# Expert tiles gathered as 32-token blocks and turned by VectorE instead of TensorE

## The chip, the cores and the metric

The kernel runs on one core of one Trainium2 chip. The metric is the time of one execution in microseconds, measured on the device. The kernel before took 2295.74 us, the median of three runs from 2294.14 to 2295.92. One execution was also recorded by the hardware profiler; the rows below come from that record.

A core has a matrix engine (TensorE, PE in the rows; PEld is its weight load), a vector engine (VectorE, DVE), a scalar engine (ScalarE, ACT), GpSimd (POOL), and SyncE (SP), which issues most DMAs. Each engine takes its instructions in a fixed order.

## The reference

An attention without softmax feeds a mixture of experts.

```python
scores = z @ z.T / S                      # B = 8 batches, S = 2496, z is 64 wide
x = u * (relu(scores) ** 2 @ v)           # D = 256
logits = x @ w_gate + modality_bias[modality_id]
e = argmax(logits); gate = softmax(logits)[e]     # E = 8 experts, N = B * S = 19968 tokens
out[token] = gate * (relu(x[token] @ w1[e]) @ w2[e])      # w1[e]: 256 x 1024, w2[e]: 1024 x 256
```

Products are made in about fp32: each operand is split into a high part in the fp32r format and a low part, the rest, and three of the four partial products are added.

## The kernel before, in words

Phase 1 (to about 1358 us) is the attention: 400 steps of scores, square, split and product with v, ordered by a planner (`beside`) that places side work on ScalarE and VectorE by estimated costs and due times. Each token's row of 256 values, with its gate weight and its token number behind it (258 words), is scattered by GpSimd into `xs` in DRAM, where every expert has a region of its own. `lay_weights` copies w1 and w2 once into DRAM scratch (`w1s`, `w2s`) in the order in which a later load wants them.

Phase 2 is the experts, in tiles of 512 rows of one expert. Tiles are numbered from -4. Tiles -4 to -1 belong to the fullest expert, so that they can start before the last tokens are routed; tiles 0 to 34 follow, then a half tile. Tile -4 is turned at the end of phase 1, the three after it by the early tile ahead of them (tile 0 by tile -1), and tile t + 1 by tile t from then on: 39 whole tiles and one half are turned in all.

- `fetch(t)` loads the tile's rows from `xs` into a buffer of SBUF with one DMA; in tile t it loads tile t + 2. `fetch_weights` loads the expert's w1 and w2 behind it on SP.
- `turn(t)` brings features onto the partitions: per half of the features four TensorE transposes (`pt`, line 794) into PSUM, a ScalarE copy to the high part `xh` (line 802), a VectorE subtraction to the low part `xl` (line 803).
- `run_tile(t)` runs f = 0 to 7 over the hidden features in slices of 128. `up(t, f)` makes six matmuls of 512 columns into one of two PSUM buffers `ph` (line 952); then ScalarE makes `hh` (line 956) and VectorE `hl` (line 957), the high and low part after the relu. `down(t, f - 2)` follows `up(t, f)` from f = 2 on (lines 965, 966). The buffer that `up(t, f)` fills is that of `up(t, f - 2)`, so it waits until `hl` of f - 2 has read it. In tiles from 0 on, `turn(t + 1)` stands behind `up(t, 1)`; in early tiles behind `up(t, 5)`.
- `finish(t)` scales by the gate (`part`, `y`) and scatters rows of the output.

In phase 2 the order on every engine is the order of the code; in phase 1 SP's order is left to the scheduler of the language.

Of the kernel before, what the change touches and what calls it, by code (L numbers as in the profile page):

```python
# [21 lines left out]
def ins_of(x):  # L22
    return getattr(x, "ins", x)
# [3 lines left out]
def tile_attention_moe(ctx: ExitStack, tc: tile.TileContext, u, v, zt, mid, wg, mb, w1, w2, out):  # L27
# [11 lines left out]
    nc = tc.nc  # L39
    B, S, D = u.shape  # L40
# [30 lines left out]
    ident_r = const.tile([P, P], F32R, name="ident")  # L71
# [8 lines left out]
    turned = ctx.enter_context(tc.tile_pool(name="turned", bufs=1))  # L80
    rows = ctx.enter_context(tc.tile_pool(name="rows", bufs=1))
# [6 lines left out]
    def bank_tile(shape, name):  # L88
        return bank["pool"].tile(shape, F32, tag=bank["tag"], name=name)
# [29 lines left out]
    n = NCOL - J  # L119
# [16 lines left out]
    def make_blank():  # L136
        t = raw.tile([P, J, XW], F32, tag="blank", name="blank")
        nc.gpsimd.memset(t, 0.0)
        nc.gpsimd.memset(t[:, :, D + 1:D + 2], NOWHERE)
        blank.append(t)  # L140

    def clear(e):
        tc.keep_in_program_order(
            nc.sync.dma_start(out=xs[e * CAP:e * CAP + T, :].rearrange("(p j) c -> p j c", j=J), in_=blank[0])
        )
# [57 lines left out]

    def lay_weights(e, n):
        if n == 0:
            nc.sync.dma_start(out=w1s[e], in_=w1[e].rearrange("(k p) f -> p k f", p=P))
        else:
            nc.sync.dma_start(out=w2s[e], in_=w2[e].rearrange("(j p) d -> p j d", p=P))

# [128 lines left out]
    def evacuate_low(b, c, h):  # L338

        w = width[c]  # L340
        if not h:
            x = rows.tile([P, J, XW], F32, tag="x", bufs=NCH + 1, name="x")
            t = x.rearrange("p j c -> p (j c)")[:, 0:KD * T].rearrange("p (k t) -> p k t", k=KD)
# [147 lines left out]
    def scatter(b, k):  # L491
# [140 lines left out]
    G = len(steps)  # L632
# [20 lines left out]

    def none(f, *args):
        return (None, 0.0, f, args)
# [38 lines left out]
    for e in range(E):  # L694
        for n in range(2):
            k = 2 * e + n
# [16 lines left out]
    TL, W, head = {}, [None] * NW, []  # L713
    ready, fetched = {"n": 0}, {"n": 0}
    data = mybir.DependencyInfo(mybir.DependencyClass.Sync, mybir.DependencyReason.DATA)

    def wait_rows(i):
        for s in scatters[ready["n"]:]:
            tc.add_manual_dep(i, s.name, data, reason="rows of tokens")
        ready["n"] = len(scatters)  # L720

    def fetch(t, r0=0, nj=J):

        n = t + EARLY
        cell = first[0:1, 1:2] if t < 0 else meta[0:1, t, 0:1]
        row = nc.sync.value_load(cell, min_val=0, max_val=(E - 1) * CAP if t < 0 else E * CAP - T)
        k = fetched["n"] % 3
        fetched["n"] += 1
        xg = head[k // 2].tile([P, J, XW], F32R, tag=f"xg{k}", name="xg")[:, 0:nj, :].bitcast(F32)
        r0 += n * T if t < 0 else 0  # L730
        src = xs[bass.ds(row + r0 if r0 else row, nj * P), :]
        i = ins_of(nc.sync.dma_start(out=xg, in_=src.rearrange("(p j) c -> p j c", j=nj)))
        wait_rows(i)
        TL[t] = xg

    def weight_tiles(pool, n):
        W[n] = (
# [47 lines left out]
        if EARLY > 1:  # L785
            fetch(1 - EARLY)

    def turn_rows(t, dh):

        xg = TL[t]  # L790
        nj = xg.shape[1]
        pt = bank_tile([P, T], "pt")[:, 0:nj * P]
        for j in range(nj):
            nc.tensor.transpose(  # L794
                out=pt[:, j * P:(j + 1) * P].bitcast(F32R),
                in_=xg[:, j, dh * P:(dh + 1) * P].bitcast(F32R),
                identity=ident_r,
            )
        return pt

    def part_rows(x, dh, pt):
        nc.scalar.copy(out=x[0][:, dh, :], in_=pt)
        nc.vector.tensor_tensor(out=x[1][:, dh, :], in0=pt, in1=x[0][:, dh, :].bitcast(F32), op=ALU.subtract)

    def turned_tiles(nj):
        return [turned.tile([P, KD, T], F32R, tag="zm", bufs=NCH + 1, name=n)[:, :, 0:nj * P] for n in ("xh", "xl")]

    def turn(t):
        x = turned_tiles(TL[t].shape[1])
        for dh in range(KD):  # L810
            part_rows(x, dh, turn_rows(t, dh))
        TL[t] = (TL[t], *x)

    first_turned = []

    def turn_early(t):
        first_turned[:] = [turn_rows(t, dh) for dh in range(KD)]

    def part_early(t):
        x = turned_tiles(J)  # L820
        for dh in range(KD):
            part_rows(x, dh, first_turned[dh])
        TL[t] = (TL[t], *x)

    at(EG + 2, begin)
    for q in range(KD + 2):
        queue(G - 8 + q, G - 4 + q, act(1.05, part_weights_high, -1, q), dve(1.25, part_weights_low, -1, q))
    at(G - 5, turn_early, -EARLY)
    queue(G - 4, G - 4, none(part_early, -EARLY))

    ET = mybir.EngineType
    for c in range(3):
# [2 lines left out]
    with tc.manual_schedule(engines={ET.PE, ET.Activation, ET.DVE, ET.Pool}):  # L835
# [47 lines left out]
        for g in range(G):  # L883
            waiting += [(end, g, p) for end, p in due.pop(g, ())]
            b, c, i = steps[g]
# [6 lines left out]
            ahead = 1 + sum(g >= n for n in DEEPER)  # L892
# [77 lines left out]
    done = []  # L970

    def finish(t, po, group):
        xg, TL[t] = TL[t][0], None
        ids = mp.tile([P, J], I32, tag="ids", bufs=3, name="ids")[:, 0:len(po)]
        nc.vector.tensor_copy(out=ids, in_=xg[:, :, D + 1])
        mine = []
        for j in range(len(po)):
            gate = xg[:, j, D:D + 1]
            part2 = mp.tile([P, D], F32, tag="part2", bufs=2, name="part2")
            nc.scalar.mul(out=part2, in_=po[j][:, D:2 * D], mul=gate)  # L980
            y = mp.tile([P, D], F32, tag="y", bufs=6, name="y")
            nc.vector.scalar_tensor_tensor(out=y, in0=po[j][:, 0:D], scalar=gate, in1=part2, op0=ALU.mult, op1=ALU.add)  # L982
            i = ins_of(
                nc.gpsimd.indirect_dma_start(  # L984
                    out=out,
                    out_offset=bass.IndirectOffsetOnAxis(ap=ids[:, j:j + 1], axis=0),
                    in_=y,
                    in_offset=None,
                    bounds_check=N - 1,
                    oob_is_err=False,  # L990
                )
            )
            tc.declare_no_dep(i, group=group, reason="a tile's tokens are distinct")
            tc.add_to_no_dep_group(group, i)
            for s in done:
                tc.add_manual_dep(i, s.name, data, reason="rows that two tiles of an expert share")
            mine.append(i)
        done[:] = mine
# [5 lines left out]
                fetch(n)  # L1004

    def run_tile(t, ahead, extra={}, part=""):
        if not isinstance(TL[t], tuple):
            turn(t)
        po = [ps_o.tile([P, 2 * D], F32, tag="o", name="po") for _ in range(TL[t][0].shape[1])]
        h = {}  # L1010
        for f in range(KF + 2):
            if f < KF:
                h[f] = up(t, f)
            if 2 <= f < KF:
                for j in range(len(po)):
                    down(t, f - 2, h[f - 2], po, j)
            if ahead and t >= -1 and 2 <= f < 2 + KD + 2:
                part_weights_high(t + 1, f - 2)
                part_weights_low(t + 1, f - 2)
            for g in extra.get(f, ()):  # L1020
                g()
            if f == (1 if t >= 0 else 5) and ahead and t + 1 in TL:
                turn(t + 1)
        for j in range(len(po)):
            for f in range(KF - 2, KF):
                down(t, f, h[f], po, j)
        finish(t, po, f"out{t}{part}")
# [10 lines left out]
    for k, pieces in ((0, (route_logits, route_exp)), (1, (route_places,)), (3, (route_count,)), (4, (route_slots, route_gates))):  # L1038
        n, f = slots[k]
# [5 lines left out]
    n, f = slots[13]  # L1045
# [15 lines left out]
    if MAXT > UNC:  # L1061
# [49 lines left out]
```

## Time and profile before

| | |
|---|---|
| median of three runs | 2295.74 us |
| the profiled execution | 2293.02 us, span 2290.8 us |
| TensorE busy | 2263.6 us, 99% of the span |
| VectorE, ScalarE busy | 77%, 69% |
| granted TensorE clock, mean | 0.997 of full speed |

The span runs from the first to the last instruction; the execution's own time has 2.2 us around it. A busy TensorE is not one at its peak: matmuls are pipelined and their recorded ends overlap, so that what a matmul costs is read from the distance of two starts.

### The profile page before, as it was taken

Reading aid. Unit: us, or ns where it says so; the run is one execution under the profiler, and the core shown is the slowest. Engines: PE = TensorE matmul, PEld = TensorE weight load, DVE = VectorE, ACT = ScalarE, POOL = GpSimd, SP = SyncE. Lnnn points to the kernel's source line nnn. Section 1 sums busy time; section 2 is a strip of 40 time slices with the busy share of each in tenths; the row PEclk is TensorE's granted clock in tenths of the full one; section 3 lists DMA queues with packets and bytes.
Section 4 is the critical chain, followed back from the end, with each engine's and each line's share of the span. In section 5 each row is a group of like instructions: output and inputs, shape, how many; then the busy total and the mean of one; then the engine's idle time right before and its main releaser. Section 6 shows DMA issues by size and latency. Waiting matters only on the chain.

```text
span 2290.8 us, 44756 instructions
## 1 busy us (share of the span) xinstructions
PE 2263.6 (99%) x17220; PEld 2022.7 (88%) x17220; DVE 1758.0 (77%) x4540; ACT 1587.7 (69%) x1966; POOL 367.1 (16%) x350
## 2 busy tenths in 40 slices
PE   9999999999999999999999999999999999999996
PEld 7888888998998998999999998888888888888885
DVE  6879989989889889889889997656565555555563
ACT  8888888888888888888888863545454545444543
POOL 0000210210220210210211313112121212121211
PEclk9999999999999999999999999999999999999998
DMA  9602112112112112112110122534343434343430
GB/s 304 227 30 68 45 49 76 38 53 71 41 52 70 47 55 61 52 50 66 47 50 30 54 92 92 175 111 165 112 156 121 153 124 150 127 141 136 137 135 25
DMA packets 101791, 216.90 MB, mean 95 GB/s; under 512 B 15488, under 2 KB 63104, under 8 KB 96704
## 3 DMA queue, kind: packets, MB, share of 16 engines
q1 hardware_dynamic: 86432, 172.61, 23.1%
q0 software_dynamic: 15136, 41.34, 4.9%
q8 instruction: 137, 2.24, 0.4%
q14 instruction: 86, 0.70, 0.1%
HBM read 168.36 MB, written 62.32 MB: 101 GB/s over the span
## 4 chain that ended last, share of the span: by engine, by line
PE 92%; DVE 3%; ACT 2%; issue 2%; DMA 0%; POOL 0%; ACTq 0%; POOLq 0%; DVEq 0%
PE acc L305 42%; PE ph L952 18%; PE po L965 12%; PE s L265 11%; PE po L966 6%; DVE spare L385 1%; PE pt L794 1%; ACT r L267 1%; PE po L363 1%; ACT r L273 0%; DVE al L289 0%; ACT vh L234 0%; ACT x L347 0%; DMA out_dram<-y,ids 0%; DVE hl L957 0%
## 5 line engine op out<-in xcount | busy, mean ns | idle before, releaser
L267 ACT ACTIVATE r<-s 128x1024 f32<-128x1024 f32 (+1 forms) x400 | 403.4, 1008 | 198.3 <-PE s L265 187.6
L289 DVE TENSOR_TENSOR al<-r,ah 128x1024 fp32r<-128x1024 f32 (+1 forms) x360 | 431.0, 1198 | 101.6 <-ACT ah L280 85.1
L305 PE MATMUL acc<-ah,vh 64*128 64x512 f32 (+1 forms) x3120 | 465.7, 384 | 0.9 <-DVE ah L280 0.9
L385 DVE SCALAR_TENSOR_TENSOR spare<-x,wgb 128x256 f32<-128x256 f32 x1280 | 462.2, 421 | 1.0
L305 PE MATMUL acc<-ah,vl 64*128 64x512 f32 (+1 forms) x3120 | 458.5, 383 | 0.0
L956 ACT ACTIVATE hh<-ph 128x512 fp32r<-128x512 f32 (+1 forms) x320 | 189.8, 593 | 385.7 <-PE ph L952 376.4
L305 PE MATMUL acc<-al,vh 64*128 64x512 f32 (+1 forms) x3120 | 456.5, 382 | 0.1
L965 PE MATMUL po<-w,hh 128*128 128x512 f32 x1264 | 452.0, 393 | 0.0
L952 PE MATMUL ph<-xh,w 128*128 128x512 f32 (+1 forms) x1280 | 446.5, 395 | 0.4 <-issue 0.4
L273 ACT ACTIVATE r<-r 128x1024 f32<-128x1024 f32 (+1 forms) x400 | 416.3, 1041 | 3.5
L957 DVE SCALAR_TENSOR_TENSOR hl<-ph,hh 128x512 fp32r<-128x512 f32 (+1 forms) x320 | 219.1, 685 | 255.3 <-ACT hh L956 251.8
L305 PEld LDWEIGHTS acc<-ah,vh 64*128 64x128 f32 x3120 | 349.8, 184 | 27.5 <-ACT x L347 1.6
L305 PEld LDWEIGHTS acc<-al,vh 64*128 64x128 f32 x3120 | 350.1, 184 | 23.1 <-DVE al L289 0.5
L498 POOL DMA_INDIRECT xs<-x,sloti x160 | 205.5, 1284 | 1027.3 <-DVE x L496 939.2
L305 PEld LDWEIGHTS acc<-ah,vl 64*128 64x128 f32 x3120 | 347.3, 184 | 24.6
L265 PE MATMUL s<-zm 64*128 64x512 f32 (+1 forms) x2400 | 363.6, 387 | 4.9 <-ACT r L267 4.4
L966 PE MATMUL po<-w,hl 128*128 128x256 f32 x1264 | 353.4, 280 | 0.5 <-DVE hl L957 0.5
L280 ACT CAST ah<-r 128x1024 fp32r<-128x1024 f32 (+1 forms) x291 | 296.0, 1017 | 0.0
L952 PEld LDWEIGHTS ph<-xh,w 128*128 128x128 f32 x1280 | 239.5, 188 | 56.6 <-DVE hl L957 1.4
L965 PEld LDWEIGHTS po<-w,hh 128*128 128x128 f32 x1264 | 237.0, 187 | 55.1
L265 PEld LDWEIGHTS s<-zm 64*128 64x128 f32 x2400 | 260.3, 185 | 24.8 <-ACT r L267 7.5
L984 POOL DMA_INDIRECT out_dram<-y,ids x158 | 154.2, 976 | 725.4 <-DVE y L982 699.7
(138 smaller groups left out, 1967.1 us busy)
## 6 DMA issues: line engine op xcount, KB each, us to landing
w<-w1s SPq DMA_DIRECT2D x37, 1024.0 KB
w<-w2s SPq DMA_DIRECT2D x37, 1024.0 KB
xg<-xs SPq DMA_DIRECT2D x39, 516.0 KB
vr<-in_v_dram SPq DMA_DIRECT2D x32, 512.0 KB
ut<-in_u_dram SPq DMA_DIRECT2D x32, 512.0 KB
zr<-in_zt_dram SPq DMA_DIRECT2D x40, 256.0 KB
w1s<-in_moe_w_dram SPq DMA_DIRECT2D x8, 1024.0 KB
w2s<-in_moe_w_dram SPq DMA_DIRECT2D x8, 1024.0 KB
```

Of the source, the lines that this page charges most:

```text
L265: nc.tensor.matmul(out=s[:, t, :w], lhsT=lhs, rhs=mv[halves[t], ql, :w], start=n == 0, stop=n == 2)
L267: nc.scalar.activation(out=r[:, :, :w], in_=s[:, :, :w], func=AF.Relu, scale=INV)
L273: nc.scalar.square(out=a[:, :, :w], in_=a[:, :, :w])
L280: copy(out=ah[:, :, :w], in_=st_a[g][:, :, :w])
L289: nc.vector.tensor_tensor(out=al[:, :, :w], in0=a[:, :, :w], in1=ah[:, :, :w].bitcast(F32), op=ALU.subtract)
L305: nc.tensor.matmul(out=acc[b, c][r][dh][:, :w], lhsT=V[b, k // J][y][halves[r], k % J, dh * P:(dh + 1) * P], rhs=x[halves[r], k % 2, :w], ...
L385: nc.vector.scalar_tensor_tensor(out=spare[:, k % 2, :], in0=x[:, j, 0:D], scalar=1.0, in1=wgb[:, e, :], op0=ALU.mult, op1=ALU.mult, accum ...
L498: nc.gpsimd.indirect_dma_start(out=xs, out_offset=bass.IndirectOffsetOnAxis(ap=RT[b]["sloti"][:n, k:k + 1], axis=0), in_=x[:n, j, :], in_o ...
L952: nc.tensor.matmul(out=ph, lhsT=lhs, rhs=rhs[:, k, :], start=n == 0, stop=n == 3 * KD - 1)
L957: nc.vector.scalar_tensor_tensor(out=hl, in0=ph, scalar=0.0, in1=hh.bitcast(F32), op0=ALU.max, op1=ALU.subtract)
L965: nc.tensor.matmul(out=po[j], lhsT=hh[:, s], rhs=both, start=f == 0, stop=False, skip_group_check=True)
L966: nc.tensor.matmul(out=po[j][:, 0:D], lhsT=hl[:, s], rhs=w[:, 0, :], start=False, stop=f == KF - 1, skip_group_check=True)
```

## The change

Each tile is gathered by five DMAs. Four load blocks: features 64 b to 64 b + 63 of token 32 t + i go to partition 32 b + i, where block t has 64 words, so that one VectorE instruction, which turns every 32 x 32 square of a 128 x 1024 operand, leaves features on partitions and tokens in their order along the row. The fifth loads gate and token number into `side`. With this a partition holds other features than before (feature 64 b + 32 k + q on partition 32 b + q), and `lay_weights` orders the rows of w1 to match, in two copies of half the size. Three instructions take the place of `turn`'s twelve: a VectorE transpose `xt`, a ScalarE copy `xh`, and a VectorE subtraction `xl`, the last two now 1024 wide and from SBUF. They stand behind `up(t, 0)` (the first two) and `up(t, 1)` in tiles from 0 on, behind `up(t, 5)` and `up(t, 6)` in early ones, and the planner places those of tile -4.

```diff
     def lay_weights(e, n):
         if n == 0:
-            nc.sync.dma_start(out=w1s[e], in_=w1[e].rearrange("(k p) f -> p k f", p=P))
+            for k in range(KD):
+                nc.sync.dma_start(
+                    out=w1s[e, :, k, :].rearrange("(b q) f -> b q f", q=BLK),
+                    in_=w1[e].rearrange("(b k q) f -> k b q f", k=KD, q=BLK)[k],
+                )
...
-        src = xs[bass.ds(row + r0 if r0 else row, nj * P), :]
-        i = ins_of(nc.sync.dma_start(out=xg, in_=src.rearrange("(p j) c -> p j c", j=nj)))
-        wait_rows(i)
-        TL[t] = xg
+        src = xs[bass.ds(row + r0 if r0 else row, nt), :]
+        dmas = []
+        for b in range(P // BLK):
+            cols = slice(b * KD * BLK, (b + 1) * KD * BLK)
+            rows_of = src[:, cols].rearrange("(t i) c -> i t c", i=BLK)
+            dmas.append(nc.sync.dma_start(out=xg[b * BLK:(b + 1) * BLK], in_=rows_of))
+        dmas.append(nc.sync.dma_start(out=side, in_=src[:, D:XW].rearrange("(j p) c -> p j c", p=P)))
...
-    def turn_rows(t, dh):
...
-    def part_rows(x, dh, pt):
-        nc.scalar.copy(out=x[0][:, dh, :], in_=pt)
-        nc.vector.tensor_tensor(out=x[1][:, dh, :], in0=pt, in1=x[0][:, dh, :].bitcast(F32), op=ALU.subtract)
...
+    def turn_blocks(t):
+        side, xg = TL[t]
+        nt = xg.shape[1] * BLK
+        xt = turned.tile([P, KD, T], F32, tag="zm", bufs=NCH + 1, name="xt")[:, :, 0:nt]
+        TL[t] = (side, xt)
+        nc.vector.transpose(
+            out=xt.rearrange("p k (t i) -> p k t i", i=BLK), in_=xg.rearrange("p t (k c) -> p k t c", k=KD)
+        )
+    def part_high(t):
+        side, xt = TL[t]
+        xh, xl = (turned.tile([P, KD, T], F32R, tag="zm", ...)[:, :, 0:xt.shape[2]] for n in ("xh", "xl"))
+        nc.scalar.copy(out=xh, in_=xt)
...
+    def part_low(t):
+        side, xh, xl, xt = TL[t]
+        nc.vector.tensor_tensor(out=xl, in0=xt, in1=xh.bitcast(F32), op=ALU.subtract)
...
-    at(G - 5, turn_early, -EARLY)
-    queue(G - 4, G - 4, none(part_early, -EARLY))
+    queue(G - 6, G - 4, dve(1.2, turn_blocks, -EARLY), act(1.05, part_high, -EARLY), dve(1.25, part_low, -EARLY))
...
-            if f == (1 if t >= 0 else 5) and ahead and t + 1 in TL:
-                turn(t + 1)
+            if ahead and t + 1 in TL:
+                if f == (0 if t >= 0 else 5):
+                    turn_blocks(t + 1)
+                    part_high(t + 1)
+                if f == (1 if t >= 0 else 6):
+                    part_low(t + 1)
```

On ScalarE, in a tile from 0 on, the order before was (`part` is the end of the tile ahead, `hh` the slices f = 0, 1, 2 of this one):

```order
L980 ACTIVATE part_23309<-po,xg 128x256
L980 ACTIVATE part_23316<-po,xg 128x256
L956 ACTIVATE hh<-ph 128x512 x2
L802 CAST xh<-pt 128x512 x2
L956 ACTIVATE hh<-ph 128x512
L770 CAST w_0_18680<-w_0_18680 128x1024
```

and it is now:

```order
L982 ACTIVATE part_23213<-po,xg 128x256
L982 ACTIVATE part_23220<-po,xg 128x256
L958 ACTIVATE hh<-ph 128x512
L816 CAST xh<-xt 128x1024
L958 ACTIVATE hh<-ph 128x512 x2
L785 CAST w_0_18688<-w_0_18688 128x1024
```

`xh` of the next tile has moved from behind `hh` of f = 1 to ahead of it.

On VectorE, in the same place, the order before was (`y` is the end of the tile ahead):

```order
L982 SCALAR_TENSOR_TENSOR y<-po,xg,part_23316 128x256
L957 SCALAR_TENSOR_TENSOR hl<-ph,hh 128x512 x2
L803 TENSOR_TENSOR xl<-pt,xh 128x512 x2
L957 SCALAR_TENSOR_TENSOR hl<-ph,hh 128x512
L774 TENSOR_TENSOR w_0_18680<-w_0_18680 128x1024
```

and it is now:

```order
L984 SCALAR_TENSOR_TENSOR y<-po,xg,part_23220 128x256
L959 SCALAR_TENSOR_TENSOR hl<-ph,hh 128x512
L809 STREAM_TRANSPOSE xt<-xg 128x1024
L959 SCALAR_TENSOR_TENSOR hl<-ph,hh 128x512
L821 TENSOR_TENSOR xl<-xt,xh 128x1024
L959 SCALAR_TENSOR_TENSOR hl<-ph,hh 128x512
```

The transpose stands between `hl` of f = 0 and `hl` of f = 1, and `xl` between those of f = 1 and f = 2.

On VectorE at the end of phase 1 the order before was (`al` and `ah` are the attention's split, `spare` the router's products, `w` the low parts of tile -4's weights):

```order
L385 SCALAR_TENSOR_TENSOR spare,lg<-x,wgb 128x256 x4
L496 COPY x<-side 128x2
L803 TENSOR_TENSOR xl<-pt,xh 128x512 x2
L291 TENSOR_TENSOR al<-r,ah 128x448
L292 TENSOR_TENSOR al<-r,ah 64x448
L385 SCALAR_TENSOR_TENSOR spare,lg<-x,wgb 128x256 x6
L774 TENSOR_TENSOR w_0_18680<-w_0_18680 128x1024 x2
```

and it is now, from the transpose on:

```order
L809 STREAM_TRANSPOSE xt<-xg 128x1024
L391 SCALAR_TENSOR_TENSOR spare,lg<-x,wgb 128x256 x2
L295 TENSOR_TENSOR al<-r,ah 128x2x448
L391 SCALAR_TENSOR_TENSOR spare,lg<-x,wgb 128x256 x6
L502 COPY x<-side 128x2
L286 CAST ah<-r 128x2x448
L297 TENSOR_TENSOR al<-r,ah 128x448
L298 TENSOR_TENSOR al<-r,ah 64x448
L391 SCALAR_TENSOR_TENSOR spare,lg<-x,wgb 128x256 x2
L789 TENSOR_TENSOR w_0_18688<-w_0_18688 128x1024
L821 TENSOR_TENSOR xl<-xt,xh 128x1024
```

Beside the transpose, one `ah` of the attention has come over from ScalarE, and eight of the router's products stand later, among tile -4's first `hl`.

## Rows read from the trace of the kernel before

**Rows 1.** The chain that ended last, share of the span by engine.

```profile
PE 92%; DVE 3%; ACT 2%; issue 2%; DMA 0%; POOL 0%; ACTq 0%; POOLq 0%; DVEq 0%
```

**Rows 2.** Stretches: length, PE, PEld, DVE, ACT, POOL busy; PEclk, DMA share, GB/s.

```profile
1338.00:1382.00 44.00, 42.27 (x321) 37.48 (x317) 42.06 (x159) 21.27 (x30) 8.60 (x8) 1.00 0.13 43
...
1700.00:1792.30 92.30, 92.30 (x482) 77.85 (x481) 54.58 (x76) 45.64 (x73) 15.61 (x16) 1.00 0.40 138
```

**Rows 3.** Timeline of PE in a tile: start us, us, what [idle before <- releaser].

```profile
1710.98 0.79 PE L794 MATMUL pt<-ident,xg 128*128 128x128 f32 x8
1711.61 0.47 PE L952 MATMUL ph<-xh,w 128*128 128x512 f32 x1
1711.91 0.40 PE L952 MATMUL ph<-xl,w 128*128 128x512 f32 x1
...
1714.47 0.39 PE L952 MATMUL ph<-xh,w 128*128 128x512 f32 x1
1714.70 0.39 PE L952 MATMUL ph<-xl,w 128*128 128x512 f32 x1
```

**Rows 4.** Timeline of ACT in the same tile.

```profile
1709.78 0.60 ACT L956 ACTIVATE hh<-ph 128x512 fp32r<-128x512 f32 x1 [0.92 <-PE ph L952]
1711.18 0.60 ACT L956 ACTIVATE hh<-ph 128x512 fp32r<-128x512 f32 x1 [0.80 <-PE ph L952]
1711.68 1.07 ACT L802 CAST xh<-pt 128x512 fp32r<-128x512 f32 x2
```

**Rows 5.** Timeline of DVE in the same tile.

```profile
1710.41 0.69 DVE L957 SCALAR_TENSOR_TENSOR hl<-ph,hh 128x512 fp32r<-128x512 f32 x1 [1.04 <-ACT hh L956]
1711.81 0.69 DVE L957 SCALAR_TENSOR_TENSOR hl<-ph,hh 128x512 fp32r<-128x512 f32 x1 [0.71 <-ACT hh L956]
1712.42 1.28 DVE L803 TENSOR_TENSOR xl<-pt,xh 128x512 fp32r<-128x512 f32 x2
```

**Rows 6.** Timeline of tile -4's end, where PE waited for hl.

```profile
1381.25 0.69 DVE L957 SCALAR_TENSOR_TENSOR hl<-ph,hh 128x512 fp32r<-128x512 f32 x1
...
1382.00 0.39 PE L966 MATMUL po<-w,hl 128*128 128x256 f32 x1 [0.48 <-DVE hl L957]
...
1382.23 0.39 PE L965 MATMUL po<-w,hh 128*128 128x512 f32 x1
```

**Rows 7.** Groups by line: shapes xcount | busy us, mean ns | idle before.

```profile
L774 DVE TENSOR_TENSOR w<-w 128x1024 fp32r<-128x1024 f32 x148 | 181.2, 1226 | 35.3 <-ACT w L770 35.1
...
L770 ACT CAST w<-w 128x1024 fp32r<-128x1024 f32 x148 | 153.9, 1042 | 0.0
...
L280 DVE CAST ah<-r 128x1024 fp32r<-128x1024 f32 (+1 forms) x109 | 73.9, 678 | 2.3 <-ACT r L273 2.2
...
L794 PE MATMUL pt<-ident,xg 128*128 128x128 f32 x316 | 31.7, 244 | 0.0
...
L444 DVE TENSOR_TENSOR_SCAN run<-reset,hot 128x160 f32<-128x160 f32 x9 | 4.4, 492 | 0.3
```

**Rows 8.** DMA queue from 16.3 to 17.5 us: packets, MB, share of 16 engines.

```profile
q1 hardware_dynamic: 1091, 0.03, 53.2%
```

**Rows 9.** DMA from 1718.5 to 1721.5 us: busy tenths in 40 slices; queue.

```profile
DMA  9999999997765544333212211111100000000000
...
q1 hardware_dynamic: 444, 0.44, 41.8%
```

**Rows 10.** Waits from 1338 to 1382.2 us: total us, times, longest.

```profile
DVE hl L957 <- ACT hh L956: 1.6, 1, 1.6
...
PE po L363 <- DVE x L351: 1.3, 1, 1.3
```

**Rows 11.** Timeline of SP: fetches of a tile, the first and last of four.

```profile
1709.40 0.33 SPq L732 DMA_DIRECT2D xg<-xs  x1
...
1778.60 0.34 SPq L732 DMA_DIRECT2D xg<-xs  x1
```

**Rows 12.** Issues of the copies into w1s: duration ns, first and last start.

```profile
L206 SPq DMA_DIRECT2D w1s<-in_moe_w_dram x8: 636/5195/8527, 21.9 to 64.0; - x8
```

More of the change, by code (lines that the diff above doesn't have):

```diff
@@ L52, in tile_attention_moe @@
     XW = D + 2
+    BLK = 32
     CAP = N
@@ L715, in tile_attention_moe, with wait_rows @@
     data = mybir.DependencyInfo(mybir.DependencyClass.Sync, mybir.DependencyReason.DATA)
-    def wait_rows(i):
+    def wait_rows(dmas):
         for s in scatters[ready["n"]:]:
-            tc.add_manual_dep(i, s.name, data, reason="rows of tokens")
+            for i in dmas:
+                tc.add_manual_dep(i, s.name, data, reason="rows of tokens")
         ready["n"] = len(scatters)
@@ L728, in fetch @@
         fetched["n"] += 1
-        xg = head[k // 2].tile([P, J, XW], F32R, tag=f"xg{k}", name="xg")[:, 0:nj, :].bitcast(F32)
+        words = head[k // 2].tile([P, J * XW], F32, tag=f"xg{k}", name="xg")
+        nt = nj * P
+        xg = words[:, 0:nt // BLK * KD * BLK].rearrange("p (t c) -> p t c", c=KD * BLK)
+        side = words[:, J * D:J * D + 2 * nj].rearrange("p (j c) -> p j c", c=2)
         r0 += n * T if t < 0 else 0
-        src = xs[bass.ds(row + r0 if r0 else row, nj * P), :]
-        i = ins_of(nc.sync.dma_start(out=xg, in_=src.rearrange("(p j) c -> p j c", j=nj)))
-        wait_rows(i)
-        TL[t] = xg
+        src = xs[bass.ds(row + r0 if r0 else row, nt), :]
[5 more added lines that the diff above has]
+        dmas.append(nc.sync.dma_start(out=side, in_=src[:, D:XW].rearrange("(j p) c -> p j c", p=P)))
+        wait_rows([ins_of(i) for i in dmas])
+        TL[t] = (side, xg)
     def weight_tiles(pool, n):
@@ L786, in begin @@
             fetch(1 - EARLY)
-    def turn_rows(t, dh):
[L790 to L799, printed above, removed]
-    def part_rows(x, dh, pt):
-        nc.scalar.copy(out=x[0][:, dh, :], in_=pt)
-        nc.vector.tensor_tensor(out=x[1][:, dh, :], in0=pt, in1=x[0][:, dh, :].bitcast(F32), op=ALU.subtract)
-    def turned_tiles(nj):
-        return [turned.tile([P, KD, T], F32R, tag="zm", bufs=NCH + 1, name=n)[:, :, 0:nj * P] for n in ("xh", "xl")]
-    def turn(t):
[L809 to L823, printed above, removed]
+    def turn_blocks(t):
[8 more added lines that the diff above has]
+        side, xt = TL[t]
+        xh, xl = (turned.tile([P, KD, T], F32R, tag="zm", bufs=NCH + 1, name=n)[:, :, 0:xt.shape[2]] for n in ("xh", "xl"))
+        nc.scalar.copy(out=xh, in_=xt)
+        TL[t] = (side, xh, xl, xt)
+    def part_low(t):
+        side, xh, xl, xt = TL[t]
+        nc.vector.tensor_tensor(out=xl, in0=xt, in1=xh.bitcast(F32), op=ALU.subtract)
+        TL[t] = (side, xh, xl)
+    def turn(t):
+        for f in (turn_blocks, part_high, part_low):
+            f(t)
     at(EG + 2, begin)
@@ L972, in finish @@
     def finish(t, po, group):
-        xg, TL[t] = TL[t][0], None
+        side, TL[t] = TL[t][0], None
         ids = mp.tile([P, J], I32, tag="ids", bufs=3, name="ids")[:, 0:len(po)]
-        nc.vector.tensor_copy(out=ids, in_=xg[:, :, D + 1])
+        nc.vector.tensor_copy(out=ids, in_=side[:, :, 1])
         mine = []
         for j in range(len(po)):
-            gate = xg[:, j, D:D + 1]
+            gate = side[:, j, 0:1]
             part2 = mp.tile([P, D], F32, tag="part2", bufs=2, name="part2")
@@ L1006, in run_tile @@
     def run_tile(t, ahead, extra={}, part=""):
-        if not isinstance(TL[t], tuple):
+        if len(TL[t]) < 3:
             turn(t)
```

## The prediction

> **What bounds the kernel now.** I read the chain that ended last first: 92% of the span is TensorE, 3% VectorE [rows 1]. So a change pays by what it takes from TensorE's stream, and costs by what it makes TensorE wait for. Then the stretches: in four tiles of phase 2 TensorE is busy for all of 92.30 us at full granted clock, VectorE for 59%, ScalarE for 49%, DMA at 0.40; in the last 44 us of phase 1 and the start of tile -4 VectorE has 42.06 of 44.00 us [rows 2]. There VectorE binds as well; elsewhere the reader sees room on all the helpers. Last, one tile in order of time on TensorE, ScalarE and VectorE [rows 3 to 5], since room on average says nothing of who waits for whom. The tile's period is 23.07 us: four fetches, the first and last 69.20 us apart [rows 11].
>
> **What goes.** Eight transposes take TensorE from 1710.98 to 1711.61, 0.63 us, and the next matmul's successor comes after 0.30 where 0.23 is usual (1714.47 to 1714.70) [rows 3]: 0.70 us a tile. There are 316 [rows 7], 39 whole tiles and one half. If nothing took their place, the 38 whole tiles turned in phase 2 and the half would give back 27 us, 1.2%.
>
> **What takes their place in tiles from 0 on.** ScalarE and VectorE keep their order, and the new `xh` now stands ahead of `hh` of f = 1 and needs the VectorE transpose, which needs `hl` of f = 0. Before, `up(2)` came 0.70 us later, and `hh` of f = 1 waited for nothing but its matmuls. I follow the chain on the clock of [rows 3 to 5], where up(0) and up(1) are unchanged:
>
> - `hh` of f = 0 starts at 1709.78 [rows 4], `hl` of f = 0 at 1710.41 [rows 5]. VectorE's next instruction can start 0.61 after such an `hl` (1711.81 to 1712.42, rows 5): the transpose starts at 1711.02.
> - The transpose of 128x1024 is an operation that the trace does not hold. [...] An element costs the subtraction 1.04 ns (1226 ns for 1024 against the 0.69 us of rows 5 for 512), which leaves 0.16 us fixed; with that the scan's 2.1 ns per element would make 2.3 us. I take 1.23: no row shows a reordering instruction at the copy's double rate, and it handles every element once, as the subtraction does. The ends kept for the range are 0.68 and 2.3.
> - It ends at 1712.25. An engine released by VectorE starts 0.06 after the end (`hl` 1381.25 + 0.69 to 1382.00, rows 6): `xh` at 1712.31.
> - `xh` takes 1.04, as the copy of the same shape for the weights [rows 7]; ScalarE's next starts 0.10 before an end (1711.18 + 0.60 to 1711.68, rows 4): `hh` of f = 1 at 1713.25, where it started at 1711.18.
> - `hl` of f = 1 comes 0.63 behind `hh` (1709.78 to 1710.41): 1713.88, and TensorE may fill the buffer 0.75 after that start [rows 6]: 1714.63. `up(3)` uses this buffer.
>
> TensorE itself would be there earlier. up(2) may start at 1710.41 + 0.75 = 1711.16 instead of 1711.61, a small new wait of 0.18; with its six matmuls (1.40), the four pairs of `down` (1.40) and 0.10 for restarting after a wait (0.23 instead of 0.12 behind 1382.00, rows 6) it reaches `up(3)` at 1714.06. It then waits 0.57 us for the buffer, and 0.10 more for the restart, so that `up(3)` runs as if started at 1714.73, against 1714.47 before [rows 3]: 0.26 us later, not 0.70 earlier. Behind that the chain has slack: `xl` fills 1.2 us of VectorE ahead of `hl` of f = 2, whose buffer is wanted 2.8 us after `up(3)`. What is queued behind the waiting `xh` on ScalarE is `hh` of f = 1, and TensorE waits for it: this is the step that decides. Tiles 0 to 33 turn a whole tile: 34 x 0.26 = +8.8 us. Tile 34 turns a half, with a transpose of about 0.69 and an `xh` of 0.59, so that the buffer is free in time: -0.4.
>
> [...]
>
> **Early tiles.** Tiles -3 to -1 turn the next one behind `up(5)` (so does tile -4, counted below). No `up` follows that needs the buffer of f = 6, and `down` of f = 6 comes after up(7) and eight matmul pairs, so the cover holds and the 0.70 us stays won: -2.1.
>
> **The end of phase 1.** Where VectorE is full, it gets two transposes (1.14 each in steps), one `ah` of about 0.65 that the planner moved over, and saves 0.06 at each `xl`: +2.8 us. Of this the 1.6 us that VectorE idled for `hh` [rows 10] can be refilled, by the eight router products that now stand there; TensorE, which lost 1.3 us to `x` of line 351 [rows 10], loses more or less with it. Bounds +1.2 and +2.8; I take +2.0.
>
> **The gather.** A tile's fetch becomes 2048 pieces of 256 bytes and 512 of 8 bytes, 160 for each of 16 DMA engines. The trace has no 256-byte piece. Pieces of 32 bytes cost 0.532 x 16 x 1.2 / 1091 = 9.4 ns of an engine [rows 8], of 1 KB 0.418 x 16 x 3.0 / 444 = 45 ns [rows 9]: 1.5 to 7.2 us per tile, on the line between them 2.5. DMA is busy for 0.40 x 23.07 = 9.2 us of a tile [rows 2], old fetch included, and goes quiet by 1721 [rows 9], twelve us before the next one. The transpose of a tile runs over 24 us after its fetch was issued (1709.40, rows 11). SP issues five DMAs where it issued one, some 2 us more, and the weights queued behind it move by that and by the pieces, at most 9 us, inside these twelve. So I cost the gather at nothing; the cover is gone when a piece costs more than (23.07 - 9.2) / 160 = 87 ns.
>
> **The weights' layout** moves the same bytes in 16 copies of half the size. Before, all eight were issued in the crowded first 64 us [rows 12]; SP now has them between later loads. I cost it at nothing.
>
> **Sum.** +8.8 - 0.4 - 2.1 + 2.0 = +8.3 us on the profiled execution's 2293.0, of which 2.2 lie around the span: 2301.3. The median of the runs is 2.7 above that execution, so a median of 2304.0, 0.4% slower. The likeliest case's own range: 0.10 us of a tile's chain is 3.4 us, a transpose of 1.13 to 1.35 us is 3.4 to 4 us, the boundary 0.8: 2298 to 2311.
>
> **The rivals.**
>
> 1. *The transpose runs at the copy's rate (faster).* Place: the same link from `hl` of f = 0 to `xh`. At 0.68 us `xh` starts at 1711.76 and the buffer is free at 1714.08, when TensorE arrives: `up(3)` comes 0.39 earlier, 34 x 0.39 = -13.3, and the boundary costs about 1 less: 2293.0 - 14.8 + 2.7 = 2281. It decides from a transpose under 0.97 us on, where before and after are equal. For it: one source in SBUF, as the copy. Against: every element crosses partitions. [...] Chance 0.13.
> 2. *The transpose is much slower than a subtraction,* up to the scan's 2.3 us: 34 x (2.3 - 0.97) = 45, and 2 more at the boundary: 2342. Only the scan speaks for it. Chance 0.09.
> 3. *The gather becomes the bound.* If a piece cost 100 ns, DMA would need 9.2 + 16 = 25.2 us per tile, 2.1 over the period, 38 times: 2376. Against it stand both rows of pieces. [...] Chance 0.03.
> 4. *Copies into w1s hold up loads of phase 1.* Each of the eight took a median of 5.2 us to issue [rows 12]; if TensorE waited once for each of 16, 83 us. Against: loads have buffers to run ahead, and DMA is at 0.13 at the end of the phase [rows 2]. Most would be hidden: 2295 to 2330. Chance 0.03.
>
> **Chances.** The forecast has 0.72. The range reaches down to rival 1 and up until about a tenth is out: 2280 to 2318. A change under 0.2%, 4.6 us, is no change for a measurement of this kernel, whose three runs lie within 0.08%. Slower: most of the forecast (a transpose under 1.11 us, or a chain 0.1 us shorter, leaves it within 4.6 us) and rivals 2 to 4, 0.72. Faster: rival 1 and a shorter chain than I read, 0.15. The same: 0.13.
>
> **What would show it.** Right: a transpose near 1.23 us; in tiles from 0 on a wait of `up(3)` for `hl` of about 0.6 us, `hh` of f = 1 starting about 2 us later against `up(1)` than before, a period of 23.3 us, and 22.4 in tiles -3 to -1. Wrong: TensorE without gaps in the tile; `xt` waiting for a DMA; TensorE waiting for `ah` or `s` in phase 1 because of a late load; a transpose far from 1.23.

## The result, and the profile after

The changed kernel takes 2306.84 us (median of five runs, 2304.0 to 2307.63), the kernel before 2295.16 (2293.55 to 2295.92) on the same chip: a ratio of 1.0047, 95% interval 1.0034 to 1.0059. It is slower by 0.5%; 2304.0 had been predicted. The profiled executions are 2304.23 (span 2302.5) and 2293.02: 11.2 us apart, and it is these that are accounted for below.

First the chain that ended last, in shares of the span by engine.

```profile
PE 84%; ACT 6%; DVE 4%; issue 4%; DMA 0%; POOL 0%; POOLq 0%; DVEq 0%; ACTq 0%
```

TensorE's share went from 92% [rows 1] to 84%, and ScalarE's from 2% to 6%: the chain now leaves TensorE in the tiles from 0 on. The stretches show the same (length, PE, PEld, DVE, ACT, POOL busy, granted clock, DMA share, GB/s); the third holds tile -3.

```profile
1338.00:1382.00 44.00, 40.39 (x304) 35.86 (x301) 41.80 (x150) 20.31 (x27) 7.71 (x8) 1.00 0.28 61
1700.00:1792.30 92.30, 90.68 (x445) 74.07 (x444) 56.55 (x76) 44.16 (x69) 15.57 (x16) 1.00 0.45 134
1387.00:1411.00 24.00, 23.01 (x115) 18.90 (x114) 17.97 (x63) 8.25 (x15) 7.99 (x8) 1.00 0.23 61
```

Where nothing was idle before [rows 2], TensorE now lacks 1.6 us of 92.30, and 44.00 us at the end of phase 1 have 40.39 where they had 42.27. The new operations, by line and shape (count, busy us, mean ns, idle before):

```profile
L809 DVE STREAM_TRANSPOSE xt<-xg 128x1024 f32<-128x1024 f32 x39 | 48.2, 1235 | 0.0
...
L821 DVE TENSOR_TENSOR xl<-xt,xh 128x1024 fp32r<-128x1024 f32 x39 | 47.4, 1216 | 0.0
...
L816 ACT CAST xh<-xt 128x1024 fp32r<-128x1024 f32 x39 | 40.9, 1049 | 76.9 <-issue 61.1 <-DVE xt L809 15.8
```

The transpose takes 1235 ns, and the copy `xh` finds ScalarE waiting 76.9 us in all. The view puts 61.1 of them down to "issue", for which it names no releaser; but in every tile from -3 on `xh` starts 0.03 to 0.04 us after the transpose ends, so it is the transpose each time. It is the same place in a tile as [rows 3 to 5], 5.57 us later by the clock of the trace (`hh` of f = 0 at 1715.35, before at 1709.78). ScalarE, VectorE and TensorE in turn:

```profile
1715.35 0.60 ACT L958 ACTIVATE hh<-ph 128x512 fp32r<-128x512 f32 x1 [0.93 <-PE ph L954]
1717.85 1.05 ACT L816 CAST xh<-xt 128x1024 fp32r<-128x1024 f32 x1 [1.91 <-issue]
1718.80 1.08 ACT L958 ACTIVATE hh<-ph 128x512 fp32r<-128x512 f32 x2
```

```profile
1715.97 0.69 DVE L959 SCALAR_TENSOR_TENSOR hl<-ph,hh 128x512 fp32r<-128x512 f32 x1 [1.04 <-ACT hh L958]
1716.58 1.23 DVE L809 STREAM_TRANSPOSE xt<-xg 128x1024 f32<-128x1024 f32 x1
1719.43 0.69 DVE L959 SCALAR_TENSOR_TENSOR hl<-ph,hh 128x512 fp32r<-128x512 f32 x1 [1.61 <-ACT hh L958]
```

```profile
1716.31 0.90 PE L954 MATMUL ph<-xh,w 128*128 128x512 f32 x2
...
1719.49 0.28 PE L968 MATMUL po<-w,hl 128*128 128x256 f32 x1
1720.17 0.50 PE L954 MATMUL ph<-xh,w 128*128 128x512 f32 x1 [0.40 <-DVE hl L959]
1720.51 0.39 PE L954 MATMUL ph<-xl,w 128*128 128x512 f32 x1
```

`xt` ends at 1717.81 and `xh` starts 0.04 later; `hh` of f = 1 (the first of the "x2") at 1718.80, 2.05 later against `up(1)` than before; `hl` of f = 1 at 1719.43; up(3) at 1720.17, after a wait of 0.40. The long 0.90 at 1716.31 holds the small wait of up(2). (The 0.40 is counted from the recorded end of the matmul ahead, 1719.77. Counted by starts, the next matmul would have come 0.12 after 1719.49, so that up(3) is 0.56 late.)

How this adds up is read from the first `hh` of each tile, which ScalarE starts when `up(0)` is done; in every tile of both kernels ScalarE has been waiting for that. Two of its rows, tiles 0 and 34:

```profile
1459.06 0.60 ACT L958 ACTIVATE hh<-ph 128x512 fp32r<-128x512 f32 x1 [0.92 <-PE ph L954]
...
2251.40 0.60 ACT L958 ACTIVATE hh<-ph 128x512 fp32r<-128x512 f32 x1 [0.93 <-PE ph L954]
```

| first `hh` of tile | before | after | lag |
|---|---|---|---|
| -4 | 1359.94 | 1358.92 | -1.02 |
| -3 | 1385.91 | 1389.00 | +3.09 |
| -2 | 1409.42 | 1413.08 | +3.66 |
| -1 | 1432.73 | 1435.67 | +2.94 |
| 0 | 1456.02 | 1459.06 | +3.04 |
| 34 | 2240.26 | 2251.40 | +11.14 |
| half tile | 2262.31 | 2273.37 | +11.06 |

Three of the 11 us are there at the end of tile -4, nothing comes in tiles -3 to -1 together, and 8.10 come in tiles 0 to 33, 0.24 in each. TensorE's waits from 1338 to 2280 us (total, times, longest):

```profile
PE ph L954 <- DVE hl L959: 15.1, 35, 1.9
PE po L968 <- DVE hl L959: 4.2, 4, 2.5
PE po L369 <- DVE x L357: 1.5, 1, 1.5
```

34 of the 35 in the first row are up(3)'s 0.4, one in each of tiles 0 to 33. The 35th, 1.9 us, is up(2) of tile -4. The second row is the early tiles, where before a wait of 0.48 stood [rows 6]. At tile -4 (VectorE, TensorE, VectorE, TensorE):

```profile
1363.78 1.28 DVE L959 SCALAR_TENSOR_TENSOR hl<-ph,hh 128x512 fp32r<-128x512 f32 x2
1364.52 0.50 PE L954 MATMUL ph<-xh,w 128*128 128x512 f32 x1 [1.89 <-DVE hl L959]
...
1381.23 0.69 DVE L959 SCALAR_TENSOR_TENSOR hl<-ph,hh 128x512 fp32r<-128x512 f32 x1 [1.61 <-ACT hh L958]
1385.08 0.39 PE L968 MATMUL po<-w,hl 128*128 128x256 f32 x1 [2.49 <-DVE hl L959]
```

The eight router products that were put off stand ahead of the first two `hl`, so that up(2) waits for `hl` of f = 0. At the tile's end VectorE idles for `hh` of f = 6. In tile -3 (VectorE, ScalarE, TensorE):

```profile
1403.12 1.25 DVE L809 STREAM_TRANSPOSE xt<-xg 128x1024 f32<-128x1024 f32 x1
1405.97 0.69 DVE L959 SCALAR_TENSOR_TENSOR hl<-ph,hh 128x512 fp32r<-128x512 f32 x1 [1.61 <-ACT hh L958]
...
1407.31 1.20 DVE L821 TENSOR_TENSOR xl<-xt,xh 128x1024 fp32r<-128x1024 f32 x1
1408.44 0.67 DVE L959 SCALAR_TENSOR_TENSOR hl<-ph,hh 128x512 fp32r<-128x512 f32 x1
```

```profile
1404.40 1.05 ACT L816 CAST xh<-xt 128x1024 fp32r<-128x1024 f32 x1 [3.13 <-DVE xt L809]
1405.35 0.59 ACT L958 ACTIVATE hh<-ph 128x512 fp32r<-128x512 f32 x1
```

```profile
1409.16 0.39 PE L968 MATMUL po<-w,hl 128*128 128x256 f32 x1 [0.98 <-DVE hl L959]
```

`hh` of f = 6 stands behind `xh`, `hl` of f = 7 behind `xl`, and the `down` of f = 7 at the tile's end waits for it, 0.98 us here and 2.49 in tile -4.

### The profile page after: what moved, and what is told of

The parts are those of the page before. It is cut to its first block, busy times and chain, and to the rows that moved or that the text cites. A ratio compares the mean times of both kernels' runs of the same rounds, so it can differ in the third digit from the quotient of the medians.

```text
span 2302.5 us, 44510 instructions
## 1 busy us (share of the span) xinstructions
PE 2255.0 (98%) x16904; PEld 1993.8 (87%) x16904; DVE 1788.6 (78%) x4541; ACT 1580.7 (69%) x1925; POOL 366.2 (16%) x350
## 4 chain that ended last, share of the span: by engine, by line
PE 84%; ACT 6%; DVE 4%; issue 4%; DMA 0%; POOL 0%; POOLq 0%; DVEq 0%; ACTq 0%
PE acc L311 42%; PE ph L954 14%; PE s L271 11%; PE po L967 10%; PE po L968 5%; DVE hl L959 2%; ACT hh L958 2%; ACT xh L816 2%; ACT r L273 1%; DVE spare L391 1%; PE po L369 1%; ACT r L279 0%; DVE al L295 0%; DMA out_dram<-y,ids 0%; ACT vh L240 0%
## 5 line engine op out<-in xcount | busy, mean ns | idle before, releaser
L954 PE MATMUL ph<-xh,w 128*128 128x512 f32 (+1 forms) x1280 | 451.2, 398 | 16.1 <-DVE hl L959 15.1
```

The lines of the kernel that those rows point to most:

```text
L954: nc.tensor.matmul(out=ph, lhsT=lhs, rhs=rhs[:, k, :], start=n == 0, stop=n == 3 * KD - 1)
```

## The experiments

My theory: what is lost comes from the order on ScalarE and VectorE, `hh` of one f behind the next tile's `xh`, and reaches TensorE through the PSUM buffer that up(3) needs. The rivals: the gather and its DMA queues, the layout of w1s, or VectorE's time as such.

**1. `xh` behind `hh` of f = 1.**

```diff
                 if f == (0 if t >= 0 else 5):
                     turn_blocks(t + 1)
+                if f == (1 if t >= 0 else 5):
                     part_high(t + 1)
```

> In tiles from 0 on, `xh` is issued behind `hh` of f = 1 instead of ahead of it; nothing else changes. Theory (the changed kernel loses in these tiles only because `hh` of f = 1 stands behind `xh` and the VectorE transpose, so that up(3) gets its PSUM buffer late): up(3) no longer waits, only the small wait of up(2) for `hl` of f = 0 (0.2 us and the restart) stays, the period of a tile falls from 23.30 to 22.5 to 22.65 us, and the profiled time from 2304 to 2277 to 2282. Rival (the gather or the DMA queues set the period): it stays at 23.3 and the time at 2304 to 2307.

Measured: 2283.96 us (2283.8 to 2284.77), ratio to before 0.9954 (0.9939 to 0.9969); the profiled execution 2284.77. In tiles 0 to 33 the period is 22.65 us, where the changed kernel has 23.30; TensorE's 34 waits for the buffer are gone. So the order of two instructions decides whether the change loses 0.5% or gains 0.5%. The total is 2.8 us above the upper end of what was expected although the period fits: from the first `hh` of tile -4 to that of tile -3, where the code is the same, it took 32.80 us instead of 30.08. The stretches at its end, columns as before, show why:

```profile
1376.00:1384.00 8.00, 6.89 (x34) 5.34 (x33) 6.39 (x26) 2.03 (x3) 0.00 (x0) 1.00 0.00 0
1384.00:1392.00 8.00, 6.39 (x19) 5.39 (x20) 4.93 (x13) 1.96 (x5) 2.74 (x3) 0.57 0.10 33
1392.00:1400.00 8.00, 7.99 (x40) 6.38 (x40) 4.58 (x14) 2.39 (x4) 1.14 (x2) 1.00 0.48 99
```

With the 2.5 us wait at the end of tile -4 (to 1385.61) the granted clock falls: it is 0.57 in the mean of 8 us, and 0.50 of full speed from 1386 to 1390. There TensorE makes 8 matmuls in each 2 us, where it makes 11 to 13 from 1394 to 1404, at 1.00. In the changed kernel's profile the same wait was followed by 1.00.

**2. Four buffers for `ph`, order as changed.**

```diff
-        ph = ps_h.tile([P, T], F32, tag="h", name="ph")[:, 0:nt]
+        if t >= 0 and f % 4 > 1:
+            ph = bank_tile([P, T], "ph")[:, 0:nt]
+        else:
+            ph = ps_h.tile([P, T], F32, tag="h", name="ph")[:, 0:nt]
```

> The order of the changed kernel stays, but in tiles from 0 on `ph` has four PSUM buffers (the two that the transposes no longer use serve f = 2, 3, 6, 7). Theory: `hh` of f = 1 is as late as before, but nobody waits for its buffer until up(5), and up(2) doesn't wait for `hl` of f = 0 either: period 22.37 us (23.07 less the 0.70 of the transposes), profiled time 2272 to 2275. Rival (the late `hh` and `hl` are wanted by `down` as well, or DMA sets the pace): little or no gain, 2300 to 2307.

Measured: 2274.22 us (2270.98 to 2274.88), ratio 0.9908 (0.9893 to 0.9923), profiled 2274.05, and this with the slow stretch ahead of tile -3 again (32.70 us from tile -4's first `hh` to tile -3's). The period is 22.36: the whole 0.70 of the transposes is won. The stretch of four tiles:

```profile
1700.00:1792.30 92.30, 92.30 (x464) 77.57 (x463) 57.79 (x77) 45.71 (x70) 15.57 (x16) 1.00 0.46 138
```

TensorE has no gap, while `hl` of f = 1 is as late as in the changed kernel (1734.46, 3.45 after that of f = 0; there 1719.43, 3.46 after). At this lateness the instruction costs only through the buffer.

**3. The gather in pieces of 1 KB.**

```diff
-        for b in range(P // BLK):
-            cols = slice(b * KD * BLK, (b + 1) * KD * BLK)
-            rows_of = src[:, cols].rearrange("(t i) c -> i t c", i=BLK)
-            dmas.append(nc.sync.dma_start(out=xg[b * BLK:(b + 1) * BLK], in_=rows_of))
+        rows = words[:, 0:nj * D].rearrange("p (j c) -> p j c", c=D)
+        dmas.append(nc.sync.dma_start(out=rows, in_=src[:, 0:D].rearrange("(p j) c -> p j c", j=nj)))
```

> The changed kernel, with the 1024 bytes of a row fetched as one piece into one partition (512 pieces of 1 KB in one DMA, where four DMAs brought 2048 pieces of 256 bytes); the 8-byte pieces of gate and id stay. The tiles then hold other tokens' elements than the computation wants; instructions, buffers and waits are the same. Theory (the gather is hidden): no change, within 3 us of the changed kernel, DMA share of a tile back from 0.45 to about 0.40. Rival (the gather costs the 11 us): 2293 to 2296.

Measured: 2306.72 us (2304.06 to 2308.1), the changed kernel's time. Its four tiles:

```profile
1700.00:1792.30 92.30, 90.91 (x446) 74.20 (x445) 56.49 (x76) 44.20 (x68) 15.61 (x16) 1.00 0.40 133
```

The DMA share falls from 0.45 to 0.40 and TensorE's gaps stay. The gather works the queues harder and costs no time.

**4. Every transpose twice, order as changed.**

```diff
+        for _ in range(2):
             nc.vector.transpose(
                 out=xt.rearrange("p k (t i) -> p k t i", i=BLK), in_=xg.rearrange("p t (k c) -> p k t c", k=KD)
             )
```

> The changed kernel, with every VectorE transpose issued twice. Theory (the transpose lies in the chain that up(3) waits for, at its full length): 1.23 us or a little more for each of the 34 tiles, +42 to +44, and 2 to 5 us for the early tiles and the end of phase 1: 2348 to 2354. Rival (VectorE has 40% of room in a tile, so that 1.23 us more of it are hidden): 2304 to 2312.

Measured: 2360.21 us (2359.46 and 2360.97). The period is 24.59, 1.286 more than with one transpose: 34 tiles make +43.7, as expected. The wait of up(3) carries it:

```profile
1722.22 0.50 PE L955 MATMUL ph<-xh,w 128*128 128x512 f32 x1 [1.68 <-DVE hl L960]
```

0.40 + 1.28 = 1.68. The early part cost more than the 2 to 5 us I gave it, and so the total missed: tile -3 starts 7.8 us later than in the changed kernel, of which 2.3 were there when tile -4 started, and tiles -3 to -1 take 3.3 more. Stretches at a lower granted clock are among them (0.59 from 1364 to 1372 us, 0.73 from 1390 to 1396).

**5. Early tiles spread.**

```diff
-                if f == (0 if t >= 0 else 5):
-                    turn_blocks(t + 1)
-                    part_high(t + 1)
-                if f == (1 if t >= 0 else 6):
-                    part_low(t + 1)
+                if f == (0 if t >= 0 else 5):
+                    turn_blocks(t + 1)
+                if f == (0 if t >= 0 else 6):
+                    part_high(t + 1)
+                if f == (1 if t >= 0 else 7):
+                    part_low(t + 1)
```

> The changed kernel, but in the early tiles -4 to -1 the three steps for the next tile are spread: transpose behind f = 5 as before, `xh` behind `hh` of f = 6, `xl` behind `hl` of f = 7. Tiles from 0 on stay as they are. [...] Rival (VectorE has too much routing work there, in whatever order): within 1 us of the changed kernel, 2304 to 2308.

Measured: 2300.82 us (2299.71 to 2302.83), ratio 1.0029 (1.0018 to 1.0039), 6 below the changed kernel's median. My theory gave 2299 to 2302: the waits at the end of tiles -4, -3 and -1 (2.49, 0.98 and 0.52 us) come from `hh` of f = 6 behind `xh` and `hl` of f = 7 behind `xl`, and go, 4 to 5 us, with the stretch at the lower granted clock (0.57 in run 1) that followed the first of them in some executions. TensorE's waits over the same stretch:

```profile
PE ph L954 <- DVE hl L959: 15.6, 36, 1.9
PE po L369 <- DVE x L357: 1.5, 1, 1.5
```

The row of `down` is gone. ScalarE and VectorE in tile -3:

```profile
1403.50 0.60 ACT L958 ACTIVATE hh<-ph 128x512 fp32r<-128x512 f32 x1 [2.19 <-PE ph L954]
1404.44 1.05 ACT L816 CAST xh<-xt 128x1024 fp32r<-128x1024 f32 x1 [0.35 <-DVE xt L809]
```

```profile
1403.17 1.25 DVE L809 STREAM_TRANSPOSE xt<-xg 128x1024 f32<-128x1024 f32 x1
1404.34 0.65 DVE L959 SCALAR_TENSOR_TENSOR hl<-ph,hh 128x512 fp32r<-128x512 f32 x1
```

`hh` of f = 6 runs beside the transpose instead of behind `xh`. By the first `hh`, tiles -3 to -1 take 68.00 us; they took 70.07 in the changed kernel and 70.11 before. Tile -4 takes 27.53, where the changed kernel has 30.08. That is 4.6 us, as expected; the rest of the 6 between the medians may come from the two levels that the last section describes, which is not shown.

**6. w1s laid out as before.**

```diff
-            for k in range(KD):
-                nc.sync.dma_start(
-                    out=w1s[e, :, k, :].rearrange("(b q) f -> b q f", q=BLK),
-                    in_=w1[e].rearrange("(b k q) f -> k b q f", k=KD, q=BLK)[k],
-                )
+            nc.sync.dma_start(out=w1s[e], in_=w1[e].rearrange("(k p) f -> p k f", p=P))
```

> The changed kernel, with the rows of w1s laid out in one copy per expert as before the change (the first layer then multiplies with weights whose rows don't match the tokens' elements); everything else is the same. Theory (the layout costs nothing): 2304 to 2308, as the changed kernel. Rival (the two copies per expert hold up loads of phase 1): faster by what they cost; the two kernels are 0.15 us apart at 1330 us in their profiles, so that more than 1 us would be a surprise.

Measured: 2306.63 us (2304.31 to 2307.32). The layout costs nothing.

**7. Four buffers, `xh` behind `hh`, early tiles spread** (edits 1, 2 and 5 together).

> Four PSUM buffers for `ph` in tiles from 0 on, with `xh` behind `hh` of f = 1 there, and the early tiles spread as in the run before. Theory: the gains add: a tile of 22.37 us from 0 on, and 4 to 5 us at the early tiles; 2264 to 2269. Rival (the early waits come back as others): 2271 to 2274, as with four buffers alone.

Measured: 2268.03 us (2266.83 to 2269.35), ratio 0.9884 (0.9869 to 0.9899). The gains add; this is the fastest version. Its period is 22.36, tiles -3 to -1 take 68.00.

**8. Four buffers and every transpose twice** (edits 2 and 4 together).

> Four buffers for `ph` in tiles from 0 on, order of the changed kernel, and every VectorE transpose issued twice. Theory (the transpose costs only through the buffer that up(3) waits for): in tiles from 0 on the second transpose costs nothing, period 22.4 us; at the end of phase 1 and in the early tiles it costs what it cost with two buffers, 8 to 11 us: 2281 to 2286. Rival (VectorE's time itself counts): 34 times 1.23 us more, about 2316 or above.

Measured: one execution of 2301.69 us, and a profiled one of 4517.88, in which the matmuls of one group took 658 ns instead of 383 (last section); nothing is concluded from that one. 2302 was neither answer, so the kernel ran again, with the step that had been overlooked written down first.

> The run of four buffers and doubled transposes once more: its profiled execution ran at half speed from end to end and took 4518 us, the other 2302, above the 2281 to 2286 that were expected. What was overlooked: with four buffers the next to want the late `hl` of f = 1 is `down` of f = 1. In the profile of four buffers that `hl` starts at 1734.46 and the first `down` matmul that reads it at 1736.01; 1.24 later it is there only at about 1736.45. Theory: a wait of about 0.45 us (and 0.10 for the restart) of `down` for `hl` in each of 34 tiles, period 22.9 us, 2298 to 2304. Rival (VectorE's time itself counts): a period of 23.6 and 2316 or above.

Measured: 2301.64 us (2300.7 to 2303.03), period 22.96. TensorE's waits from 1340 to 2280 us:

```profile
PE po L972 <- DVE hl L963: 14.2, 41, 2.5
...
PE ph L958 <- DVE hl L963: 1.9, 1, 1.9
```

The wait has moved from `ph`, where up(3) stood, to `po`, where `down` of f = 1 reads `hl`. An order that hides 1.2 us needn't hide 2.5.

**9. Every transpose twice, in the version of 7.**

> Every VectorE transpose issued twice, in the kernel with four buffers, `xh` behind `hh` of f = 1, and spread early tiles. Theory (once neither the buffer nor `down` of f = 1 waits behind it, the second transpose is hidden, because VectorE is busy for only 60 to 65% of a tile): period 22.4 us in tiles from 0 on; only the end of phase 1 and tile -4, where VectorE has no room, cost 2 to 5 us: 2268 to 2274. Rival (VectorE's time itself counts): 34 times 1.23 us, 2309 or above.

Measured: 2271.28 us (2270.93 and 2271.62), ratio 0.9903 (0.9874 to 0.9931). The period stays at 22.36. Its four tiles:

```profile
1700.00:1792.30 92.30, 92.30 (x467) 77.72 (x466) 62.91 (x84) 46.22 (x71) 15.61 (x16) 1.00 0.46 138
```

VectorE does 3.3 us more than in run 7's stretch (59.66), and TensorE has no gap. The same second transpose costs 53 us in the order of the change, 27 with four buffers, and 3 with the order mended too. In the tiles from 0 on, what counts is what waits behind an instruction of VectorE, and not its time as such; at the end of phase 1 and in tile -4, where the 3 us arise, VectorE has no room (42.22 us busy of the 44.00 from 1338 to 1382).

## Why the prediction was right, and which of its steps weren't

- **The chain in tiles from 0 on: right, step by step.** Moved by the 5.57 us between the two traces, the prediction reads: transpose at 1716.59, `xh` 1717.88, `hh` 1718.82, `hl` 1719.45, buffer free 1720.20, second matmul of up(3) at about 1720.53. The trace has 1716.58, 1717.85, 1718.80, 1719.43, 1720.17 and 1720.51. The wait of up(3), 0.57 predicted, is 0.56 by starts. Predicted +0.26 a tile, measured +0.24 (23.304 against 23.066 us) in each of the 34: +8.1 for +8.8.
- **The transpose's price: right.** 1.23 taken, 1235 ns measured. Rivals 1 and 2 needed 0.68 and 2.3, from the copy's 678 ns and the scan's 492 ns for 160 elements [rows 7]. Run 4 shows that the price is paid in full on this chain (1.286 us a tile for the second transpose), as both rivals assumed.
- **Tile 34: small and nothing.** -0.4 predicted, -0.06 measured: it takes 21.98 against 22.04 us from its first `hh` to the next tile's.
- **Early tiles: wrong.** "So the cover holds and the 0.70 us stays won: -2.1" came out as nothing: -0.04 for tiles -3 to -1 (70.07 against 70.11). Only tile -2 kept its 0.7 (22.59 against 23.31); in tiles -3 and -1 TensorE waited 0.98 and 0.52. I had asked who needs the buffer of f = 6 and given `down` the eight matmul pairs as cover, but had not put the chain on a clock as I did for tiles from 0 on. There two steps queue in a row: `hh` of f = 6 behind `xh`, and `hl` of f = 7 behind `xl`. Run 5 takes both away and brings tiles -3 to -1 to 68.00 us, 2.11 under before: the whole 2.1.
- **The end of phase 1: too low and by another mechanism.** +2.0 taken, bounds +1.2 and +2.8, measured +3.09 where tile -3 starts. I counted VectorE's added work and let the 1.6 us of idling be refilled by the eight router products. They did refill it, but from a place ahead of `hl` of f = 0, for which up(2) then waited 1.89. And at the end of tile -4 VectorE idled another 1.61 us for the same `hh` behind `xh`, and TensorE waited 2.49 there, where it had waited 0.48 [rows 6]. Run 5 takes this second wait away, and tile -4 with it is 2.55 shorter: without it the end of phase 1 would have cost about 0.5. The wait of 1.89 is left in run 5 and was not tested by itself.
- **The gather at nothing: right** (run 3). From the shares, 0.05 x 23.3 = 1.2 us of an engine go to 128 pieces of 256 bytes in place of 32 of 1 KB: with 45 ns for one of these [rows 9] it is about (1.2 + 32 x 0.045) / 128 = 0.02 us a piece, an estimate, far under the 87 ns at which the cover would have gone.
- **The weights' layout at nothing: right** (run 6).
- **The sum.** +8.1 for 8.8, -0.1 for -0.4, nothing for -2.1, +3.1 for 2.0: 11.1 for 8.3. Two errors at the early part, 3.2 us together, were partly offset by the steady tiles. The median was to lie 2.7 above the profile's time, as it had before; it lies 2.6 above. That was luck: the profile was again of the lower of the two levels in the last section, and in runs 3 and 6, whose profiles are of the upper, the median lies 0.4 and 0.0 above.

## What to carry to other kernels

An instruction on a helper engine is priced by what stands behind it in that engine's queue: the same second transpose cost 53, 27 and 3 us here. Put the chain of one tile on a clock, with each queue's order and each buffer's next user, for every kind of tile: where that was done here the numbers came out within 0.03 us, where it was argued in a sentence, for the early tiles, the whole gain of 2.1 us was missing. When a prefetch step must wait for another engine, issue it behind the evictions that TensorE waits for; here that, and two PSUM buffers that lay idle, made the same work 1.7% faster (2306.8 to 2268.0 us) with no instruction removed.

## What the runs showed of the hardware that I had not expected

- **Two levels of one kernel's time.** The changed kernel's five runs stand at 2304.0 and 2304.2, and at 2306.8 to 2307.6; before, and runs 3, 6 and 7, have two such groups as well. The profiles that were taken of the upper group (runs 3, 6 and 7) have a granted clock of 0.66 from 10 to 15 us, in the start of phase 1, those of the lower group (before and after) 1.00. Run 5's profile, the longest of its eight executions, and run 4's have 0.66 there too. Run 6's profile is one of the upper:

```profile
10.00:15.00 5.00, 4.71 (x28) 3.83 (x30) 4.30 (x6) 3.54 (x5) 0.00 (x0) 0.66 1.01 409
```

  TensorE makes 28 matmuls in these 5 us, where the changed kernel makes 44. The clock records of the kernels before and after hold two values, 1.00 and, from 2277.6 and 2288.2 us to the end, 0.50; with these two, 0.66 is 0.50 for about 3.4 of the 5 us, an estimate. TensorE had also been slower before them: from 0 to 5 us run 6 has 16 matmuls in 3.52 us of busy time and the changed kernel 18 in 3.53, and from 5 to 10 us 20 in 3.31 against 26 in 3.03. Run 6 starts tile -4 2.1 us after the changed kernel, most of the 2.4 between the two profiles' times. What decides which level an execution takes is not shown.
- **A wait that sometimes costs twice.** The 2.5 us wait at the end of tile -4 was followed by 1.00 in the changed kernel's profile and by nearly 7 us at 0.50 in runs 1 and 2 (means of 2 us from 1384 to 1392: 0.70, 0.50, 0.50, 0.60 in run 1 and 0.60, 0.50, 0.50, 0.70 in run 2), which made tile -3 start 2.6 to 2.7 us later. What decides between the two is not shown. In run 5, without the wait, the clock stays at 1.00 there (in all stretches of 2 us from 1360 to 1404).
- **An execution at half speed, with no reading of its clock** (run 8): 4517.88 us against 2301.69. The group of one phase 1 matmul in its profile (busy us, mean ns, idle before), which takes 383 ns in the changed kernel's:

```profile
L311 PE MATMUL acc<-ah,vh 64*128 64x512 f32 (+1 forms) x3120 | 825.3, 658 | 0.2 <-DVE ah L286 0.2
```

  Its views show a granted clock of 1.00 throughout, but its trace holds no record of the clock at all (its page has no line `PEclk`), and a stretch without a record is shown as 1.00. The kernel before has such a stretch at its start: its first record begins at 4.3 us. From 2 to 4 us (first two lines) its matmuls of 512 columns take 653 ns beside a clock shown as 1.00; from 4.8 to 5.4 us (last line) the same ones take 391:

```profile
2.00:4.00 2.00, 2.00 (x12) 1.54 (x10) 0.00 (x0) 0.36 (x2) 0.36 (x2) 1.00 0.87 312
L839 PE MATMUL warm<-zeros 64*128 64x512 f32 x12 | 2.9, 653 | 1.5 <-DVE zeros L94 1.5
...
L839 PE MATMUL warm<-zeros 64*128 64x512 f32 x8 | 1.1, 391 | 0.0
```

  So the 658 ns of run 8 would fit a granted clock of 0.50 from end to end; that is argued from the durations and not shown. The kernel ran normally in each of six other executions.
